# Forming the even heads of six groups like the odd ones in an attention kernel that shares its core with a Fourier layer

## The chip, the cores and the metric

One core of a Trainium2 chip runs the whole program. The metric is device time in microseconds (us), the median of several executions; a profile is one further execution, taken with the hardware profiler on. TensorE is written PE, VectorE DVE, ScalarE ACT, GpSimd POOL; SP is SyncE, which here does nothing but issue DMAs, in order.

## What is computed

Two independent layers, concatenated on the last axis. Part A is an attention with a compressive memory: 32 heads of width 18, four segments of 512 rows. Part B is a Fourier layer written as four dense products with DFT matrices.

```python
for s in range(N):                       # 4 segments of L = 512 rows
    logits = einsum("bhqd,bhkd->bhqk", qs, ks) * scale + mask     # causal
    p = softmax(logits)
    a_dot = einsum("bhqk,bhkd->bhqd", p, vs)
    a_mem = (phi(qs) @ M) / (phi(qs) @ z + 1e-6)
    outs.append(g * a_mem + (1 - g) * a_dot)
    M, z = M + phi(ks)^T @ vs, z + sum(phi(ks))
o = concat(outs) @ wo
a, b = x @ Re(Wd)^T, x @ Im(Wd)^T        # part B
y = Re(Ws) @ a - Im(Ws) @ b
```

## The kernel before, in words

All products keep nearly fp32 precision by splitting operands into a high and a low part. The program has three stages. In the first (about 0 to 240 us) the four segments are projected: q and k go to DRAM as three bf16 parts (`qd`, `kd`), v as `vd`, the memory's answer as `amd` (segments 1 to 3; `project_v` L309, `lookup` L390). In the second (about 240 to 930 us) two streams run side by side: `attention()` (L1138) and `dense()` (L668, the DFT products, matmuls at L583 and L628 to L633). In the third the output projection runs (`output_stage`, L868).

**Attention.** The 32 heads times 4 segments are 128 pieces, called heads here, numbered n, in 32 groups G of four (`G, h = divmod(n, 4)`); one group has one load of q and k stacks (`stack_load`), of values (`value_load`, L494) and of memory answers (`memory_load`, L1129). Scores of a head are four causal blocks of rows of 512, 384, 256 and 128 columns, 1280 in all. Heads come in pairs, an even one and an odd one, and the two are formed differently:

- An **even** head is formed *turned*. `s_fill` (L967) computes its scores in three parts (kinds 0: 512 columns; 1: 128 and 384; 2: 256) only so that DVE finds each row's maximum (`smallest`, L961, line L964). For the two even heads of a group POOL splits the maxima into three bf16 rows (`maxima`, L1005), PE turns them by an identity matmul (`maxima_transpose`, L1013, matmul L1015), ACT copies them (L1017), and two small DMAs put them as extra rows into the q stack. Then `t_fill` (L1021, matmuls L1032, L1035, L1040, L1041) computes the scores a second time, with keys on the partitions and the maximum already subtracted; ACT takes exp to fp16 (`hi`, L1044) and fp32 (`f`, L1045), POOL masks the diagonal blocks (`t_mask`, L1049), ACT copies the masked part to fp16 (`t_hi`, L1054), and DVE and POOL form the rest `lo` (`t_lo`, L1059). The result has the layout that the value product `pv` (L1061) needs.
- An **odd** head is formed *row by row*: `f_fill` (L973) computes the scores once and finds the maxima; `f_exp` (L980) adds a constant to the bias on ACT (L984) and takes exp with the row's bias (L987); `f_split_hi` (L989, L994) copies to fp16 on ACT; `f_split_lo` (L996, L998) forms the rest, 768 columns on POOL and 512 on DVE; `f_turn` (L1000, L1003) turns the 20 blocks of 128x128 with one DMA transpose issued by SP.

**Order.** Every engine runs its instructions in program order, and that order is written by hand. Iteration p of `attention()` has eight slots (L1153 to L1200, separated by `yield SLOTS[i]`; slot i below is the code ahead of the i-th yield, slot 0 the first). It handles the maxima of even head 2p, `t_fill` of even head 2(p-3), `f_fill` of odd head 2(p-2)+1, and `pv` of the heads of pair p-4. After every slot the main loop (L1209) takes as many pieces of the dense stream as keep the two streams at the same share of their planned totals; the plan's numbers (`SLOTS`) are fixed. `later(n, ...)` puts a DMA or a small step n slots on.

| slot | before: attention work in program order |
|---|---|
| 0 | `t_lo` part 0 of pair p-4; odd head: `f_exp` 2, `f_split_hi` |
| 1 | `s_fill` 0; `t_fill` 0 and 1 (and, every second iteration, the turned maxima in the columns that `t_fill` 1 leaves free); odd `f_split_lo` on POOL |
| 2 | `s_fill` 1; odd `f_split_lo` on DVE |
| 3 | `pv` of the even head; `s_fill` 2; `t_mask` |
| 4 | odd `f_fill` 1; `t_fill` 2; odd `f_fill` 0; `maxima` |
| 5 | odd `f_turn`; `stack_load`; copies in DRAM; `t_hi` |
| 6 | `pv` of the odd head; odd `f_fill` 2, `f_exp` 1; `t_lo` 1 and 2 |
| 7 | odd `f_exp` 0; `pv_out` |

**PSUM.** Score tiles use four banks in two pairs, `t` and `s`, each pair used in turn (`bank`, L564). `t_fill` 0, 1, 2 and the odd `f_fill` 0 take the `t` banks, `s_fill` 0, 1, 2 and the odd `f_fill` 1, 2 the `s` banks. A bank is free again when ACT has read it (for `s_fill`, DVE). The dense stream has three banks `d`; ACT copies finished ones out (L651, L634), and ACT and POOL also split each loaded DFT chunk (`c_cut`, L444: ACT L451, POOL L456).

Of the kernel before, what the change touches and what calls it, by code (L numbers as in the profile page):

```python
# [12 lines left out]
F32 = mybir.dt.float32  # L13
F32R = mybir.dt.float32r
F16 = mybir.dt.float16
# [20 lines left out]
COPIES = ((0, 3, 2, 0), (1, 3, 2, 2), (0, 5, 1, 0), (1, 5, 1, 1))  # L36
COPY_ROWS = 144


@with_exitstack  # L40
def infini_attention_and_fnet(ctx: ExitStack, tc: tile.TileContext, xT, wqk, w8, wv, wo, beta, xtT, cT, hT, out):
# [9 lines left out]
    kd = [dram.tile([D, 6, L], BF16, name=f"kd{s}") for s in range(NSEG)]  # L51
    vd = [dram.tile([P, 4, 8, 220], BF16, name=f"vd{s}") for s in range(NSEG)]
    amd = [dram.tile([4, P, D], F32, name=f"amd{s}") for s in range(NSEG)]
    yd = [dram.tile([P, D], F32, name=f"yd{t}") for t in range(NT)]
# [254 lines left out]
    def project_v(s, j, meanwhile):  # L309
# [26 lines left out]
        pool.tensor_tensor(vs[:, :, 0:18], r, vs[:, :, 36:54], OP.subtract)  # L336
        later(1, dma, vd[s][:, j], vs.rearrange("p (g h) c -> p g (h c)", g=8))

# [51 lines left out]
    def lookup(s, j):  # L390
# [26 lines left out]
        pool.tensor_tensor(am, nd[:, :, :DH], w.to_broadcast([P, H, DH]), OP.mult)  # L417
        later(1, dma, amd[s][j], am.rearrange("p h d -> p (h d)"))
        yield
# [73 lines left out]

    def value_load(G):  # L494
        if G < NG:
            s, g8 = divmod(G, 8)
            VS[G] = sa.tile([P, 4, 220], BF16, name="vst", bufs=2)
            dma(VS[G], vd[s][:, :, g8])

# [196 lines left out]
    def right_operands():  # L696
# [108 lines left out]
        for t, tag in ((1, "phi"), (9, "plo")):  # L805
            at(67, 4, o_load, t, lambda tag=tag: sa.tile([P, 5, P], F32, name="oraw", tag=tag, bufs=2))
        at(67, 4, lambda: list(left(0)))
# [165 lines left out]
    def f_fill(n, kind):  # L973
        o = scores(n, kind, "s" if kind else "t")
        if kind == 1:
            F_[n] = [sa.tile([P, 4], F32, name="nb", bufs=2), sa.tile([P, 1280], F32, name="pf", bufs=3), {}]
        smallest(o, kind, -SCALE, F_[n][0])
        F_[n][2][kind] = o
# [10 lines left out]
    def f_split_hi(n):  # L989
        f = F_[n][1]  # L990
        hl = sa.tile([P, 2, 1280], F16, name="hl", bufs=2)
        F_[n][2] = hl
        for a, b in ((512, 1280), (0, 512)):
            act.activation(hl[:, 0, a:b], f[:, a:b], AF.Copy)  # L994
# [5 lines left out]
    def f_turn(n):  # L1000
        hl = F_.pop(n)[2]
        PT[n] = sa.tile([P, 20, P], F16, name="ptt", bufs=2)
        nc.sync.dma_start_transpose(PT[n], hl.rearrange("p a c -> p (a c)"))  # L1003
# [17 lines left out]
    def t_fill(n, kind, maxima_of=None):  # L1021
        G, h = divmod(n, 4)
        q, k = qs_bufs[G % 4][:NPAIR + 3, h], ks_bufs[G % 4][:NPAIR + 3, h]
        if kind == 0:
            PT[n] = (sa.tile([P, 1280], F16, name="phi", bufs=2), sa.tile([P, 1280], F16, name="plo", bufs=2),
                     sa.tile([P, 1280], F32, name="pf", bufs=3))
        hi, lo, f = PT[n]
# [33 lines left out]
    def pv(n):  # L1061
# [4 lines left out]
        for i in range(4):  # L1066
            o = PV[n // 2][:, (h % 2 * 4 + i) * 55:(h % 2 * 4 + i + 1) * 55]
            for j in range(i + 1):
                if h % 2:
# [59 lines left out]
    def memory_load(G):  # L1129
        if 8 <= G < NG:  # L1130
            s, g8 = divmod(G, 8)
            dma(OG[G % 2], amd[s][:, :, 72 * g8:72 * g8 + 72].rearrange("q p c -> p q c"))

    F_LAG, T_LAG, V_LAG = 2, 3, 4
    NP = 2 * NG
    SLOTS = (1060.0, 890.0, 1060.0, 660.0, 890.0, 1060.0, 650.0, 1210.0)

    def attention():  # L1138
        for p in range(NP + V_LAG):
            def even(lag, fn, *a):  # L1140
                if 0 <= p - lag < NP:
                    fn(2 * (p - lag), *a)

            def odd(lag, fn, *a):
# [33 lines left out]
            odd(F_LAG, f_fill, 0)  # L1178
            if p % 2 and p < NP:
                maxima(p // 2)  # L1180
# [95 lines left out]
```

## Time and profile before

| | |
|---|---|
| median of 3 runs | 993.28 us (992.91 to 994.52) |
| the profiled execution's own time | 994.13 us |
| its span, first to last instruction | 992.4 us |
| granted TensorE clock | 0.999 |
| DMA moved | 209.97 MB, 212 GB/s |
| HBM read, written | 122.37 MB, 58.98 MB |

How to read it: the profile is of one execution on one core. "Busy" is the time in which an engine had an instruction in flight; matmuls overlap, so what one costs PE is seen from start to start and not from its duration. The 40 digits are tenths of busy time in equal slices of 24.8 us. "DMA share" is the mean time that the packets of the 16 DMA engines took, over the length of the stretch; it can go over 1, as packets overlap. A row of the timeline has start, length, engine, line, operation, output <- input, shapes, and in brackets the idle time before it with what ended that. A row of waits has the total, the number and the longest.

### The profile page before, as it was taken

The numbers are of one execution on the slowest core, as the hardware profiler recorded it, in microseconds if no ns is written. First come the engines' busy times: TensorE is split into PE (matmuls) and PEld (weight loads), VectorE is DVE, ScalarE is ACT, GpSimd is POOL, SyncE is SP. The second block draws the span as 40 slices with busy tenths as digits, with TensorE's granted clock in tenths as the row PEclk, the third lists the DMA queues.
The fourth block names the chain that finished last, engine by engine and source line by source line (L and its number), as shares of the span: only waits on it lengthen the run. The fifth ranks groups of instructions, "written<-read, shape, count | busy, mean of one in ns | idle before, by whom it ended". The sixth has DMA issues, their size and how long they took to land.

```text
span 992.4 us, 25495 instructions
## 1 busy us (share of the span) xinstructions
PE 980.9 (99%) x9246; PEld 918.3 (93%) x9246; DVE 786.4 (79%) x2115; ACT 714.7 (72%) x1687; POOL 675.2 (68%) x744
## 2 busy tenths in 40 slices
PE   9999999999999999999999999999999999999998
PEld 8988989898999999999999999999999999999998
DVE  6657668584678787887898878888888898989985
ACT  6757576563888777877878788886777778788442
POOL 2657576686676667676775777767676667887561
PEclk9999999999999999999999999999999999999999
DMA  7537556777578898899999998779999999988663
GB/s 241 191 117 244 194 170 241 238 243 214 146 179 206 224 239 227 203 226 241 223 253 242 235 211 191 187 196 218 247 231 219 224 241 252 249 200 180 168 199 112
DMA packets 304351, 209.97 MB, mean 212 GB/s; under 512 B 204992, under 2 KB 259136, under 8 KB 304192
## 3 DMA queue, kind: packets, MB, share of 16 engines
q1 hardware_dynamic: 304000, 208.20, 80.9%
q8 instruction: 72, 1.18, 0.5%
q14 instruction: 55, 0.45, 0.1%
q10 hardware_dynamic: 224, 0.14, 0.0%
HBM read 122.37 MB, written 58.98 MB: 183 GB/s over the span
## 4 chain that ended last, share of the span: by engine, by line
PE 84%; DVE 7%; ACT 4%; DMA 2%; issue 2%; POOL 1%; SPq 0%; POOLq 0%; DVEq 0%; ACTq 0%
PE d L583 38%; PE s L958 7%; PE v L84 4%; PE pv L1076 4%; PE qk L250 4%; PE d L628 3%; PE d L629 3%; PE d L630 3%; PE t L861 2%; PE pv L1077 2%; PE m L363 1%; PE d L861 1%; PE s L861 1%; PE t L1032 1%; PE qk L84 1%
## 5 line engine op out<-in xcount | busy, mean ns | idle before, releaser
L964 DVE CUSTOM_DVE_ANT_0 s<-s,causal 128x128 f32<-128x128 f32 (+3 forms) x512 | 248.4, 503 | 94.2 <-PE s L958 85.0
L456 POOL TENSOR_TENSOR clo<-craw,chi 128x512 fp32r<-128x512 f32 x158 | 218.2, 1381 | 91.1 <-ACT chi L451 60.8
L583 PE MATMUL d<-wide,chi 128*128 128x288 f32 x1408 | 261.9, 303 | 0.2 <-DVE y L653 0.2
L583 PEld LDWEIGHTS d<-wide,chi 128*128 128x128 f32 x1408 | 210.6, 188 | 2.7 <-issue 0.7
L583 PE MATMUL d<-wide,clo 128*128 128x288 f32 x704 | 173.4, 313 | 0.0
L998 POOL TENSOR_TENSOR hl<-pf,hl 128x768 f16<-128x768 f32 x64 | 114.0, 1782 | 67.4 <-ACT hl L994 55.6
L958 PE MATMUL s<-ks,qs 108*128 108x128 bf16 (+3 forms) x512 | 132.9, 303 | 1.7 <-DVE negm L964 1.2
L1044 ACT ACTIVATE phi<-t 128x384 f16<-128x384 f32 x128 | 61.8, 483 | 100.1 <-PE t L1041 100.1
L987 ACT ACTIVATE pf<-s,nb 128x128 f32<-128x128 f32 (+3 forms) x256 | 128.3, 527 | 6.2
L583 PE MATMUL d<-ab,chi 128*128 128x288 f32 x640 | 123.3, 302 | 0.0
L1059 DVE TENSOR_TENSOR plo<-pf,phi 128x384 f16<-128x384 f32 (+1 forms) x128 | 122.3, 955 | 0.0
L583 PEld LDWEIGHTS d<-wide,clo 128*128 128x128 f32 x704 | 117.8, 189 | 1.4
L1045 ACT ACTIVATE pf<-t 128x384 f32<-128x384 f32 (+1 forms) x192 | 99.6, 519 | 6.6 <-PE t L1032 6.3
L451 ACT ACTIVATE chi<-craw 128x512 fp32r<-128x512 f32 x160 | 100.1, 626 | 4.0 <-DMA craw<-xtT 2.4
L583 PEld LDWEIGHTS d<-ab,chi 128*128 128x128 f32 x640 | 97.8, 188 | 0.5
L994 ACT ACTIVATE hl<-pf 128x768 f16<-128x768 f32 (+1 forms) x128 | 87.4, 729 | 2.0
L583 PE MATMUL d<-ab,clo 128*128 128x288 f32 x320 | 83.0, 308 | 0.0
L628 PE MATMUL d<-wide,chi 128*128 128x288 f32 x256 | 81.4, 318 | 0.0
L630 PE MATMUL d<-wide,clo 128*128 128x288 f32 x256 | 75.6, 296 | 0.9 <-POOL clo L456 0.9
L629 PE MATMUL d<-wide,chi 128*128 128x288 f32 x256 | 75.6, 295 | 0.0
L1059 POOL TENSOR_TENSOR plo<-pf,phi 128x384 f16<-128x384 f32 x64 | 61.7, 963 | 12.0 <-ACT pf L1045 9.1
L998 DVE TENSOR_TENSOR hl<-pf,hl 128x512 f16<-128x512 f32 x64 | 69.2, 1081 | 0.0
(285 smaller groups left out, 2521.9 us busy)
## 6 DMA issues: line engine op xcount, KB each, us to landing
craw<-cT SPq DMA_DIRECT2D x128, 256.0 KB
ks<-kd SPq DMA_DIRECT2D x32, 432.0 KB
qs<-qd SPq DMA_DIRECT2D x32, 432.0 KB
craw<-xtT SPq DMA_DIRECT2D x32, 320.0 KB
vd<-vs SPq DMA_DIRECT2D x16, 440.0 KB
vst<-vd SPq DMA_DIRECT2D x32, 220.0 KB
qd<-p SPq DMA_DIRECT2D x16, 384.0 KB
kd<-p SPq DMA_DIRECT2D x16, 384.0 KB
```

The source lines that it names most:

```text
L451: act.activation(hi, raw[:, :4], AF.Copy)
L456: engine.tensor_tensor(lo, raw[:, :4], hi.bitcast(F32), OP.subtract)
L583: pe.matmul(o[h], a, b[:, h * 288:h * 288 + 288], start=start, stop=stop)
L628: pe.matmul(o, xh[:, k], wl[k][:, cs], start=k == 0, stop=False)
L629: pe.matmul(o, xh[:, k], wh[k][:, cs], start=False, stop=False)
L630: pe.matmul(o, xl[:, k], wh[k][:, cs], start=False, stop=False)
L958: pe.matmul(o[:, c:c + w], q[:, i * P:w], k[:, :w], start=True, stop=True)
L964: dve.tensor_tensor_reduce(o[:, c:c + w], o[:, c:c + w], CAUSAL[0][:, L - w:], scale=scale, scalar=-LOWEST, op0=OP.add, op1=OP.min, accum_ ...
L987: act.activation(f[:, FIRST_COL[i]:FIRST_COL[i] + w], o[:, c:c + w], AF.Exp, bias=nb[:, i:i + 1], scale=-1.0)
L998: engine.tensor_tensor(hl[:, 1, a:b], f[:, a:b], hl[:, 0, a:b], OP.subtract)
L1045: act.activation(f[:, r:r + w], o[:, :w], AF.Exp, bias=LIFT, scale=SCALE)
L1059: (pool if kind == 2 else dve).tensor_tensor(lo[:, a:b], f[:, a:b], hi[:, a:b], OP.subtract)
```

## The change

For the even heads of six of the 32 groups (G = 1, 3, 5, 7, 16, 18; twelve heads) the row-by-row way takes the place of the turned one. `s_fill`, `maxima`, `maxima_transpose`, `t_fill`, `t_mask`, `t_hi`, `t_lo` are not run for them; `f_fill`, `f_exp`, `f_split_hi`, `f_split_lo` and `f_turn` are, in iteration p = n/2 + 3, in the `t` banks alone. `pv` of such a head moves from slot 3 to slot 6. The following turned group's maxima, which stood beside `t_fill` 1 in slot 1, now stand beside the 256 columns of the new `f_fill` 2 in slot 4. The fp16 parts `phi` and `plo` become one tile, which also takes the DMA transpose of these heads. `vd` (segments 0 to 2) and `amd` (segments 1 and 2) are laid out so that a group's load is one contiguous piece per partition; the stores get eight pieces per partition instead of one.

```diff
+ROWWISE_GROUPS = (1, 3, 5, 7, 16, 18)
...
-    vd = [dram.tile([P, 4, 8, 220], BF16, name=f"vd{s}") for s in range(NSEG)]
-    amd = [dram.tile([4, P, D], F32, name=f"amd{s}") for s in range(NSEG)]
+    vd = [dram.tile([P, 8, 4, 220] if s < 3 else [P, 4, 8, 220], BF16, name=f"vd{s}") for s in range(NSEG)]
+    amd = [dram.tile([P, 8, 4, 72] if s < 3 else [4, P, D], F32, name=f"amd{s}") for s in range(NSEG)]
...
     def f_fill(n, kind):
-        o = scores(n, kind, "s" if kind else "t")
-        if kind == 1:
+        o = scores(n, kind, "s" if kind and n % 2 else "t")
+        if n not in F_:
...
     def f_split_hi(n):
         f = F_[n][1]
-        hl = sa.tile([P, 2, 1280], F16, name="hl", bufs=2)
+        hl = (sa.tile([P, 2, 1280], F16, name="hl", bufs=2) if n % 2
+              else sa.tile([P, 2, 1280], F16, name="hle", tag="pf", bufs=3))
...
-        PT[n] = sa.tile([P, 20, P], F16, name="ptt", bufs=2)
+        PT[n] = sa.tile([P, 20, P], F16, name="ptt", tag="ptt" if n % 2 else "phl", bufs=2)
...
-            even(T_LAG + 1, t_lo, 0)
+            turned(T_LAG + 1, t_lo, 0)
             odd(F_LAG + 1, f_exp, 2)
             odd(F_LAG + 1, f_split_hi)
             yield SLOTS[0]
-            G = p // 2 - 1 if p % 2 == 0 and 0 < p <= NP else None
-            even(0, s_fill, 0)
-            even(T_LAG, t_fill, 0)
-            even(T_LAG, t_fill, 1, G)
+            rowwise(T_LAG + 1, f_turn)
+            rowwise(T_LAG, f_fill, 0)
+            rowwise(T_LAG, f_fill, 1)
+            G = p // 2 - 1 if p % 2 == 0 and 0 < p <= NP and p // 2 - 1 not in ROWWISE_GROUPS else None
+            turned(0, s_fill, 0)
+            turned(T_LAG, t_fill, 0)
+            turned(T_LAG, t_fill, 1, G)
...
             odd(F_LAG + 1, f_split_lo, pool, 512, 1280)
             yield SLOTS[1]
-            even(0, s_fill, 1)
+            turned(0, s_fill, 1)
             odd(F_LAG + 1, f_split_lo, dve, 0, 512)
+            rowwise(T_LAG, f_exp, 0)
             yield SLOTS[2]
-            even(V_LAG, pv)
-            even(0, s_fill, 2)
-            even(T_LAG, t_mask)
+            turned(V_LAG, pv)
+            turned(0, s_fill, 2)
+            turned(T_LAG, t_mask)
+            rowwise(T_LAG, f_exp, 1)
             yield SLOTS[3]
             odd(F_LAG, f_fill, 1)
-            even(T_LAG, t_fill, 2)
+            turned(T_LAG, t_fill, 2)
+            rowwise(T_LAG, f_fill, 2)
+            if G is not None and 2 * (p - T_LAG) in ROWWISE:
+                maxima_transpose(G, F_[2 * (p - T_LAG)][2][2])
             odd(F_LAG, f_fill, 0)
-            if p % 2 and p < NP:
+            if p % 2 and p < NP and p // 2 not in ROWWISE_GROUPS:
                 maxima(p // 2)
             yield SLOTS[4]
...
-            even(T_LAG, t_hi)
+            turned(T_LAG, t_hi)
+            rowwise(T_LAG, f_exp, 2)
+            rowwise(T_LAG, f_split_hi)
             yield SLOTS[5]
+            rowwise(V_LAG, pv)
             odd(V_LAG, pv)
             odd(F_LAG, f_fill, 2)
+            rowwise(T_LAG, f_split_lo, pool, 512, 1280)
+            rowwise(T_LAG, f_split_lo, dve, 0, 512)
             odd(F_LAG, f_exp, 1)
-            even(T_LAG, t_lo, 1)
-            even(T_LAG, t_lo, 2)
+            turned(T_LAG, t_lo, 1)
+            turned(T_LAG, t_lo, 2)
             yield SLOTS[6]
```

`turned(...)` calls its function for even heads outside the six groups, `rowwise(...)` for those inside; `SLOTS` is unchanged.

More of the change, by code (lines that the diff above doesn't have):

```diff
@@ L336, in project_v @@
         pool.tensor_tensor(vs[:, :, 0:18], r, vs[:, :, 36:54], OP.subtract)
-        later(1, dma, vd[s][:, j], vs.rearrange("p (g h) c -> p g (h c)", g=8))
+        later(1, dma, vd[s][:, :, j] if s < 3 else vd[s][:, j], vs.rearrange("p (g h) c -> p g (h c)", g=8))
     started = set()
@@ L417, in lookup @@
         pool.tensor_tensor(am, nd[:, :, :DH], w.to_broadcast([P, H, DH]), OP.mult)
-        later(1, dma, amd[s][j], am.rearrange("p h d -> p (h d)"))
+        if s < 3:
+            later(1, dma, amd[s][:, :, j], am.rearrange("p (g h) d -> p g (h d)", g=8))
+        else:
+            later(1, dma, amd[s][j], am.rearrange("p h d -> p (h d)"))
         yield
@@ L497, in value_load @@
             VS[G] = sa.tile([P, 4, 220], BF16, name="vst", bufs=2)
-            dma(VS[G], vd[s][:, :, g8])
+            dma(VS[G], vd[s][:, g8] if s < 3 else vd[s][:, :, g8])
     for s in range(NSEG):
@@ L804, in right_operands, with second @@
                 "p a x -> p (a x)")[:, :5 * P].rearrange("p (k x) -> p k x", k=5))
-        for t, tag in ((1, "phi"), (9, "plo")):
-            at(67, 4, o_load, t, lambda tag=tag: sa.tile([P, 5, P], F32, name="oraw", tag=tag, bufs=2))
+        both = []
+        def second():
+            both.append(sa.tile([P, 2, 5, P], F32, name="oraw", tag="phl", bufs=2))
+            for i in range(2):
+                o_load(1 + 8 * i, lambda: both[0][:, i])
+        at(67, 4, second)
         at(67, 4, lambda: list(left(0)))
@@ L1024, in t_fill @@
         if kind == 0:
-            PT[n] = (sa.tile([P, 1280], F16, name="phi", bufs=2), sa.tile([P, 1280], F16, name="plo", bufs=2),
-                     sa.tile([P, 1280], F32, name="pf", bufs=3))
+            t = sa.tile([P, 2, 1280], F16, name="phl", bufs=2)
+            PT[n] = t[:, 0], t[:, 1], sa.tile([P, 1280], F32, name="pf", bufs=3)
         hi, lo, f = PT[n]
@@ L1068, in pv @@
             for j in range(i + 1):
-                if h % 2:
+                if h % 2 or n in ROWWISE:
                     b = FIRST_COL[i] // P + j
@@ L1131, in memory_load @@
             s, g8 = divmod(G, 8)
-            dma(OG[G % 2], amd[s][:, :, 72 * g8:72 * g8 + 72].rearrange("q p c -> p q c"))
+            dma(OG[G % 2], amd[s][:, g8] if s < 3 else amd[s][:, :, 72 * g8:72 * g8 + 72].rearrange("q p c -> p q c"))
     F_LAG, T_LAG, V_LAG = 2, 3, 4
     NP = 2 * NG
+    ROWWISE = {4 * G + h for G in ROWWISE_GROUPS for h in (0, 2)}
     SLOTS = (1060.0, 890.0, 1060.0, 660.0, 890.0, 1060.0, 650.0, 1210.0)
@@ L1142, in even, with turned, rowwise @@
                     fn(2 * (p - lag), *a)
+            def turned(lag, fn, *a):
+                if 2 * (p - lag) not in ROWWISE:
+                    even(lag, fn, *a)
+            def rowwise(lag, fn, *a):
+                if 2 * (p - lag) in ROWWISE:
+                    even(lag, fn, *a)
             def odd(lag, fn, *a):
```

## The prediction

> **What bounds the kernel now.** First the page's DMA digits for the whole span, then a table of stretches: PE is the bound, and in the stage where the change sits it has no idle time at all.
>
> ```profile
> DMA  7537556777578898899999998779999999988663
> ```
>
> ```profile
> 265.00:440.00 175.00, 175.00 (x1904) 164.97 (x1903) 137.32 (x413) 139.16 (x333) 122.91 (x136) 1.00 0.86 217
> 440.00:600.00 160.00, 159.95 (x1723) 150.36 (x1721) 138.83 (x401) 130.32 (x312) 114.00 (x127) 1.00 1.00 232
> 600.00:670.00 70.00, 70.00 (x735) 66.39 (x734) 56.93 (x174) 57.07 (x143) 51.05 (x59) 1.00 0.79 191
> ```
>
> The columns are PE, PE's weight loads, DVE, ACT and POOL in us (with counts), clock, DMA share, GB/s. Between 265 and 670 us, where groups 0 to 20 are formed, PE is busy 404.95 of 405 us. So time falls only by what PE no longer does, and every new wait of PE is paid in full. ACT (80 to 82%), DVE (78 to 87%) and the DMA (0.79 to 1.00) have some slack, and the waits of the same stretch say where ACT's is:
>
> ```profile
> ACT phi L1044 <- PE t L1041: 51.9, 35, 2.5
> ```
>
> An iteration takes about 10 us, so 405 us hold some forty. ACT's spare time is one gap per iteration (35 times, 1.5 us each), always ahead of `t_fill` 2 in slot 4. ACT waits there for PE: ACT is ahead of PE, by that much.
>
> **PE: what goes.** Timeline of iteration 10, PE:
>
> ```profile
> 331.20 0.39 PE L1032 MATMUL t<-qs,ks 111*128 111x128 bf16 x4
> 331.43 0.33 PE L1035 MATMUL t<-qs,ks 111*128 111x384 bf16 x1
> 331.59 0.22 PE L1015 MATMUL t<-ident,mb 128*128 128x128 bf16 x1
> 331.62 0.51 PE L583 MATMUL d<-wide,clo 128*128 128x288 f32 x2
> ...
> 333.81 0.20 PE L1076 MATMUL pv<-vst,phi 128*128 128x55 bf16 x1
> ...
> 334.33 0.27 PE L958 MATMUL s<-ks,qs 108*128 108x256 bf16 x1
> ...
> 335.20 0.22 PE L1040 MATMUL t<-qs,ks 111*128 111x128 bf16 x1
> 335.26 0.27 PE L1041 MATMUL t<-qs,ks 111*128 111x256 bf16 x1
> 335.37 0.38 PE L958 MATMUL s<-ks,qs 108*128 108x512 bf16 x1
> ```
>
> From start to start: `t_fill` 0 takes 0.23, `t_fill` 1 0.16, `t_fill` 2 0.06 + 0.11: 0.56 us for a head's 1280 columns. A changed head computes its scores once instead of twice: `f_fill` stands where `t_fill` stood, and `s_fill`, the same 1280 columns, goes. Twelve heads free 12 x 0.56 = 6.7 us; six turned maxima (L1015, 0.03 each) another 0.2. Some insertions into the dense stream vanish altogether (slots 2 and 3); no row prices that, I bound it by 0 and 1 us and take 0.1. **PE is freed of 7.0 us** (6.7 to 7.9).
>
> **ACT: what comes, and where.** The odd head in the same timeline runs just the code that the changed even heads get:
>
> ```profile
> 335.57 0.49 ACT L1044 ACTIVATE phi<-t 128x384 f16<-128x384 f32 x1 [1.41 <-PE t L1041]
> ...
> 336.91 0.62 ACT L451 ACTIVATE chi<-craw 128x512 fp32r<-128x512 f32 x1
> 337.43 0.19 ACT L984 ACTIVATE nb<-nb 128x2 f32<-128x2 f32 x1
> ...
> 338.38 0.20 ACT L984 ACTIVATE nb<-nb 128x1 f32<-128x1 f32 x1
> 338.62 0.69 ACT L987 ACTIVATE pf<-s,nb 128x512 f32<-128x512 f32 x1
> 339.34 0.20 ACT L984 ACTIVATE nb<-nb 128x1 f32<-128x1 f32 x1
> ...
> 340.08 1.37 ACT L994 ACTIVATE hl<-pf 128x768 f16<-128x768 f32 x2
> 341.36 0.62 ACT L451 ACTIVATE chi<-craw 128x512 fp32r<-128x512 f32 x1
> 341.88 0.58 ACT L1045 ACTIVATE pf<-t 128x512 f32<-128x512 f32 x1
> 342.35 0.48 ACT L1044 ACTIVATE phi<-t 128x384 f16<-128x384 f32 x1
> ```
>
> By starts: `f_exp` 1 takes 0.95, `f_exp` 0 0.83 (0.24, and 0.59 from 329.57 to 330.16 below), `f_exp` 2 0.74, `f_split_hi` 1.28, a DFT chunk's copy 0.52. A row-by-row head so costs ACT 3.8 us; a turned one costs 0.47 and twice some 0.37 in slot 1 (from 341.88) and 336.91 - 335.57 = 1.34 in slots 4 and 5, together 2.55. ACT gets 1.2 us more per changed head, against a gap of 1.5 us. In the mean this fits. But the gap lies ahead of slot 4, and the additions do not: `f_exp` 0 and 1 grow the work before it by 0.6 only, whereas `f_exp` 2 with `f_split_hi` (2.02 instead of 1.34) come behind it and ahead of the odd head's `f_exp` 1 and 0, which free PSUM banks. Nor can they start where `t_fill` 2's exps did. Those needed PE alone; `f_exp` 2 needs DVE's maximum, which in DVE's order stands behind the odd head's 128 and 384:
>
> ```profile
> 335.40 0.30 DVE L964 CUSTOM_DVE_ANT_0 s<-s,causal 128x128 f32<-128x128 f32 x1 [0.27 <-PE s L958]
> 335.79 0.57 DVE L964 CUSTOM_DVE_ANT_0 s<-s,causal 128x384 f32<-128x384 f32 x1
> 336.28 0.73 DVE L964 CUSTOM_DVE_ANT_0 s<-s,causal 128x512 f32<-128x512 f32 x1
> ...
> 338.81 0.43 DVE L964 CUSTOM_DVE_ANT_0 s<-s,causal 128x256 f32<-128x256 f32 x1 [1.39 <-PE s L958]
> ```
>
> The 256 columns would be reduced at 336.28 and ready at 336.71, not at 335.57: 1.14 us later. ACT then frees the odd `f_fill` 0's bank 1.14 + 0.68 = **1.8 us later**.
>
> *First wait: next iteration, slot 1.* Its second `t` fill needs exactly that bank. Its slack today is read twice: here `f_exp` 0 ends at 338.62 + 0.69 = 339.31 and the fill comes at 341.46; one iteration earlier 330.26 against 331.43.
>
> ```profile
> 329.57 0.69 ACT L987 ACTIVATE pf<-s,nb 128x512 f32<-128x512 f32 x1
> 330.16 0.19 ACT L984 ACTIVATE nb<-nb 128x1 f32<-128x1 f32 x1
> ...
> 341.46 0.33 PE L1035 MATMUL t<-qs,ks 111*128 111x384 bf16 x1
> ```
>
> Slack 2.15 and 1.17, against 1.8: a wait of 0 to 0.65. In the first iteration of each changed group (p = 2G + 3) the next group's turned head still has its `s_fill`, so DVE reduces twelve blocks, not eight. DVE's busy 137.32 of 175 us is 7.85 per 10; a head's reductions are, from the four rows above, 0.30 + 0.57 + 0.73 + 0.43 = 2.0: with the two `lo` parts about equal, DVE comes to 9.9 of 10 and runs up to 1 us late. Bounds 0 and 1.65; I take **0.7**, near the middle, as neither slack is rarer.
>
> *Second wait: that iteration's slot 4.* The odd `f_fill` 0 takes the bank of the changed head's `f_fill` 1. Once ACT is late, it has to do, after the odd `f_exp` 0: odd `f_exp` 2 and split (0.74 + 1.28), a chunk (0.52), `f_exp` 0 (0.83), `f_exp` 1 (0.95): 4.3 us. PE needs 335.37 - 331.43 = 3.94 for the same way today, and less after the change: `pv` of the even head, 0.52 (333.81 to 334.33), moves out of slot 3 behind slot 4, and for groups 1, 3, 5 and 16 the pair at slots 2 and 3 is itself a changed one without `s_fill` 1 and 2 (0.33). So 3.1 to 3.4: a wait of 1.2 or 0.9, none if ACT were on time and no chunk fell there. I take **1.1**. PE's faster way is what exposes ACT. In the iteration after it the moved `pv` gives ACT 0.5 us back, and the turned heads restore the gap: it ends there.
>
> Per group 1.8 us, six groups **10.8 us** (0 to 17).
>
> **DVE and POOL: what goes.** The masks, one `lo` part of 384 and the maxima leave POOL, 768 columns of `f_split_lo` come; DVE loses `t_lo` 0 and 1 for one 512 part:
>
> ```profile
> L998 POOL TENSOR_TENSOR hl<-pf,hl 128x768 f16<-128x768 f32 x64 | 114.0, 1782 | 67.4 <-ACT hl L994 55.6 <-PE t L1035 6.0 <-PE t L1015 2.7
> L1059 POOL TENSOR_TENSOR plo<-pf,phi 128x384 f16<-128x384 f32 x64 | 61.7, 963 | 12.0 <-ACT pf L1045 9.1 <-DMA y<-yd 2.5
> L998 DVE TENSOR_TENSOR hl<-pf,hl 128x512 f16<-128x512 f32 x64 | 69.2, 1081 | 0.0
> ```
>
> POOL gets 1.78 - 0.96 = 0.82 at most per head, less masks and maxima, on 122.91 busy of 175 us; PE meets both engines only through ACT. Zero.
>
> **DMA and SP.** One more transpose per changed head:
>
> ```profile
> L1003 SPq DMA_TRANSPOSE ptt<-hl x64: 3037/3745/6270, 258.7 to 918.4; - x64
> L498 SPq DMA_DIRECT2D vst<-vd x32: 595/611/1136, 227.7 to 901.6; - x32
> L94 SPq DMA_DIRECT2D vd<-vs x16: 319/320/407, 43.0 to 226.8; - x16
> ```
>
> Eight of the twelve fall between 265 and 440 us: 8 x 3.75 = 30 us on a share of 0.86 (24.5 us free) gives 1.03; four near 600 to 670 give 1.00. The stretch 440 to 600 ran at 1.00 with PE whole, so the bytes alone cost 0. The new layouts make 20 stores of the first stage shorter-pieced and 40 loads longer-pieced. A store holds SP 0.32, a load in short pieces 0.61; at twice that, 20 x 0.9 = 18 us of SP spread over 240 us in which the DMA is far from full (digits 3 to 7), so 0, with 2 us as the upper end; the loads' gain is hidden too.
>
> The new `f_turn` makes SP wait in slot 1 for `f_split_lo`; behind it in SP's order stand chunk loads, which run four chunks ahead, and the maxima's two DMAs. These start with a matmul that moves from 331.59 to about 335.4, and must land by the next `t_fill` 0, 0.22 ahead of 341.46: 5.8 us instead of 9.6 for ACT's copy, SP and the transfer. A held SP (3.75) still fits; 0, and 1 us per group as the upper end.
>
> **Sum.** 994.13 (its own time; span 992.4 and 1.7 around it) - 7.0 + 10.8 = 997.9. The median stands 0.85 below the profiled execution: **997.0**.
>
> **Rivals.** *The waits stay covered; faster.* If DVE is not late and chunks fall elsewhere, the slack of 2.15 covers the 1.8, and ACT enters slot 1 on time; of 10.8 us then 0 to 4 remain, and the time is 986 to 990.5. For it: 35 gaps of 1.5 us, and an addition of 1.2 per head. Against it: the gap is not where the addition is. It decides at a release 1.2 us later instead of 1.8.
>
> *SP becomes the bound; slower still.* Iteration 10's queue:
>
> ```profile
> 335.16 3.71 SPq L1003 DMA_TRANSPOSE ptt<-hl  x1
> ...
> 341.56 0.37 SPq L441 DMA_DIRECT2D craw<-cT  x1
> ...
> 345.11 3.10 SPq L1003 DMA_TRANSPOSE ptt<-hl  x1
> ```
>
> Six issues, the first and the last shown, stand one behind the other from 335.16 to 341.93, 6.8 of the 9.95 us to the next transpose. A second transpose makes that 10.5, more than the iteration. The even head's `f_turn` is issued in slot 1 and its `pv` stands in slot 6, some 6 us on; an issue that starts 2 us late and holds 3.75 makes PE wait 1 to 1.5 us for each changed head: 12 to 18 us more, some of it instead of ACT's waits: 1002 to 1010. The Trainium skill, Perfetto Trace Analysis, What "DMA-bound" means, counts an issuing engine whose track is solid with DMA slices as a bound of its own; at 68% of its time it is not that yet.
>
> *DVE stands behind POOL; slower still.* POOL's and DVE's parts of `f_split_lo` are issued together in slot 6. If DVE's 512 part cannot run beside POOL's 768, it ends up to 1.78 us late instead of in the row's mean of 1.08, next iteration's reductions start about 1 us later, and the first wait is 1.7 instead of 0.7: 6 us more, 1003 (1000 to 1005). Against it: the odd heads' two parts are issued within one slot of each other already, and 1.08 is their mean. The Trainium skill, SBUF — State Buffer, SBUF: two separate sides, has this as a rule: DVE with two SBUF inputs and a POOL instruction that reads SBUF exclude each other for the whole instruction.
>
> *Nothing measurable*: waits of 6 to 8 us, 991.3 to 995.3.
>
> **How the numbers follow.** Forecast (995.3 to 1001) 0.42, covered waits 0.34, SP 0.08, DVE behind POOL 0.05, evened out 0.11. A measurement of this kernel tells 0.2%, 2 us, from no change: faster 0.34, same 0.11, slower 0.55. The range: 987 leaves out a twelfth of all at the bottom (the covered case with no wait left), 1004 most of SP's and a third of DVE's; the forecast's own is 995.3 to 1001.
>
> **What would show it.** Right: PE waits at the second `f_fill` of the changed groups' second iteration and at the odd `f_fill` 0 in slot 4, released by ACT, 1 to 3 us per group, none in other iterations; the gap ahead of L1044 gone there. PE loses 12 x 7 = 84 matmuls at L1032 to L1041 and six at L1015. Wrong: PE busy whole from 265 to 670 us and the span 7 us shorter; or waits at `pv` L1076 behind the transposes (then SP); or a stall in the first stage (then the layouts).

## The result, and the profile after

The changed kernel takes **1034.8 us** (median of 4 runs, 1029.89 to 1038.45) against 993.1 us before (992.68 to 994.52): ratio 1.0414, 95% interval 1.0369 to 1.0459. It is slower, by far more than the forecast of 997.0, and above the forecast's range of 987 to 1004.

The profiled execution took 1035.5 us, its span is 1033.7: 41.3 more than before. First the page: busy time of the engines, PE's 40 digits, its granted clock, the DMA, and the chain that ended last.

```profile
PE 987.4 (96%) x9156; PEld 922.4 (89%) x9156; DVE 785.2 (76%) x2103; ACT 726.6 (70%) x1717; POOL 664.8 (64%) x708
...
PE   9989999999989797979999999989999999999998
...
PEclk9989999999999999999999999989999999999999
DMA  7647758767789989899999999969999999988653
...
PE d L587 29%; PE s L968 5%; DMA ptt<-hle 4%; PE qk L251 4%; PE pv L1087 4%; PE qk L85 3%; PE v L85 3%; PE d L634 3%; PE d L632 2%; PE d L633 2%; PE t L871 2%; DVE s L974 2%; PE pv L1088 2%; PE d L871 1%; PE s L871 1%
```

PE's digits, which were nines, now hold three 7s in slices 13 to 17 (counted from 0, so between about 336 and 465 us). PEclk shows an 8 only in slices 2 and 26, where PE's digit is an 8 as well; in a slice of 25.8 us a shorter loss of clock doesn't show. PE has 90 matmuls fewer, as foreseen (84 and 6), yet is busy 987.4 us instead of 980.9. A new entry stands in the chain: `DMA ptt<-hle`, the even heads' transposes, with 4%. The stretches that the prediction read (busy time of each engine, clock, DMA share, GB/s; the third one ends later because the groups do):

```profile
265.00:440.00 175.00, 157.48 (x1599) 147.27 (x1598) 122.30 (x366) 130.01 (x313) 104.06 (x99) 0.97 0.93 214
440.00:600.00 160.00, 153.89 (x1674) 144.49 (x1673) 128.92 (x376) 125.80 (x297) 107.37 (x117) 0.99 1.02 230
600.00:680.00 80.00, 77.62 (x802) 73.93 (x799) 64.68 (x194) 66.05 (x171) 55.33 (x61) 1.00 0.96 213
```

PE, which had no idle time here, is idle for 17.5, 6.1 and 2.4 us. The other engines are busy less in these windows because less gets done in them (1599 matmuls instead of 1904 in the first); over the whole span ACT is busy 11.9 us longer than before (726.6 against 714.7), POOL 10.4 less, DVE about as long. What PE waited for in the whole span (us in total, times, longest):

```profile
PE pv L1087 <- DMA ptt<-hle: 14.3, 6, 4.0
PE s L1026 <- DVE nb L974: 12.2, 6, 3.2
PE qk L251 <- DVE xt L120: 3.3, 1, 3.3
PE s L968 <- ACT pf L997: 3.2, 7, 0.8
PE s L968 <- DVE negm L974: 2.3, 5, 0.8
```

L1087 is `pv`, L1026 the turned maxima's matmul, L251 the first stage's projection, L968 the score matmul; of the last row 1.2 us were there before. **The balance:** idle time grew from 11.5 (992.4 - 980.9) to 46.3 us, by 34.8, and the first four rows make 33.0 of it. Busy time grew by 6.5 although 7.0 were freed, so 13.5 came to it. These 13.5 us are matmuls at half clock. The granted clock says so without the balance: at 0.986 over 1033.7 us, 14.5 us are lost; before, at 0.999 over 992.4 us, it was 1.0. Short stretches behind the waits show where:

```profile
67.00:73.00 6.00, 6.00 (x18) 4.84 (x18) 2.30 (x6) 3.54 (x10) 4.23 (x12) 0.50 0.63 157
298.47:301.88 3.41, 1.46 (x13) 1.19 (x12) 2.65 (x10) 2.15 (x8) 1.35 (x2) 1.00 0.93 226
301.88:305.29 3.41, 3.41 (x17) 3.41 (x16) 0.62 (x4) 3.25 (x9) 2.24 (x2) 0.50 0.22 70
```

PEclk is 0.50 in the first and the third row, and 1.00 a few us on; in the second row PE waits. There are six such stretches. Before the change this occurred only at the very end.

**The maxima's wait.** PE and DVE around the first of them:

```profile
298.46 0.50 PE L968 MATMUL s<-ks,qs 108*128 108x128 bf16 x3
300.92 0.22 PE L1026 MATMUL s<-ident,mb 128*128 128x128 bf16 x1 [1.95 <-DVE nb L974]
```

```profile
299.48 0.29 DVE L974 CUSTOM_DVE_ANT_0 s<-s,causal 128x128 f32<-128x128 f32 x1
...
299.86 0.57 DVE L974 CUSTOM_DVE_ANT_0 s<-s,causal 128x384 f32<-128x384 f32 x1
...
300.34 0.47 DVE L974 CUSTOM_DVE_ANT_0 s<-s,causal 128x256 f32<-128x256 f32 x1
300.72 0.14 DVE L974 DVE_READ_ACCUMULATOR2_ANT nb<- 128x1 f32 x1
```

PE fills three score blocks from 298.46 on; its next instruction in order is the maxima's matmul into the free columns of the 256-column tile. DVE reduces that tile in place, as the third block in its order (128, 384, 256), and the matmul starts at 300.92, after the maximum is read at 300.72 + 0.14. The columns differ, but the tile is one, and `f_fill` 2 with its reduction is written ahead of `maxima_transpose`. PE meets DVE here, six times, for 1.4 to 3.2 us.

**The transposes' wait.** SP's queue and PE one iteration later:

```profile
303.71 3.98 SPq L1014 DMA_TRANSPOSE ptt<-hl  x1
...
311.16 4.08 SPq L1014 DMA_TRANSPOSE ptt<-hle  x1
```

```profile
314.45 0.68 PE L587 MATMUL d<-ab,chi 128*128 128x288 f32 x4
317.00 0.20 PE L1087 MATMUL pv<-vst,ptt 128*128 128x55 bf16 x1 [1.86 <-DMA ptt<-hle]
```

The even head's transpose (311.16) stands behind the odd one and four other issues and holds SP to 315.24; `pv`, which PE could have started 1.86 us sooner, starts at 317.00. Rows of the tile `ptt` and of `vd` (count; duration in ns: least, median, most):

```profile
L1014 SPq DMA_TRANSPOSE ptt<-hl x64: 3012/3808/6871, 264.0 to 959.9; - x64
L1014 SPq DMA_TRANSPOSE ptt<-hle x12: 3648/4639/6032, 293.6 to 697.6; - x12
```

```profile
L95 SPq DMA_DIRECT2D vd<-vs x16: 319/514/1162, 42.2 to 233.4; - x16
```

A transpose of an even head holds SP for 4.6 us (median), not the 3.75 that I took; a `vd` store in shorter pieces 0.51 instead of 0.32.

**Where ACT waits** between 265 and 670 us:

```profile
ACT phl L1055 <- PE t L1052: 28.2, 20, 2.5
ACT nb L994 <- DVE nb L974: 23.7, 10, 4.4
```

The gap ahead of `t_fill` 2 fell from 51.9 us in 35 to 28.2 in 20; each is still 1.4 us long, but the changed heads have no `t_fill` 2. ACT now waits for DVE's maxima as well, the forecast's mechanism. But it reaches PE only through the fourth row above, 3.2 us. Three of its seven waits stand at the forecast's first place, the second fill of slot 1 (294.53, 342.79 and 390.98, for 0.61, 0.31 and 0.32 us); none stands at the second, the odd `f_fill` 0 of the same iteration, which comes right behind the maxima's matmul.

### The profile page after: what moved, and what is told of

Read it like the earlier page. It is cut to its first block, busy times and chain, and to the rows that moved or that the text cites. A ratio compares the mean times of both kernels' runs of the same rounds, so it can differ in the third digit from the quotient of the medians.

```text
span 1033.7 us, 25339 instructions
## 1 busy us (share of the span) xinstructions
PE 987.4 (96%) x9156; PEld 922.4 (89%) x9156; DVE 785.2 (76%) x2103; ACT 726.6 (70%) x1717; POOL 664.8 (64%) x708
## 4 chain that ended last, share of the span: by engine, by line
PE 68%; DVE 10%; DMA 9%; ACT 5%; issue 4%; POOL 2%; SPq 1%; POOLq 0%; DVEq 0%; ACTq 0%
PE d L587 29%; PE s L968 5%; DMA ptt<-hle 4%; PE qk L251 4%; PE pv L1087 4%; PE qk L85 3%; PE v L85 3%; PE d L634 3%; PE d L632 2%; PE d L633 2%; PE t L871 2%; DVE s L974 2%; PE pv L1088 2%; PE d L871 1%; PE s L871 1%
## 5 line engine op out<-in xcount | busy, mean ns | idle before, releaser
L587 PEld LDWEIGHTS d<-wide,chi 128*128 128x128 f32 x1408 | 214.3, 191 | 3.9 <-DVE y L657 0.9
L997 ACT ACTIVATE pf<-s,nb 128x128 f32<-128x128 f32 (+3 forms) x304 | 152.4, 527 | 8.2
L968 PE MATMUL s<-ks,qs 108*128 108x128 bf16 (+3 forms) x512 | 128.6, 303 | 6.0 <-ACT pf L997 3.2
L1055 ACT ACTIVATE phl<-t 128x384 f16<-128x384 f32 x104 | 50.4, 484 | 77.0 <-PE t L1052 77.0
L1070 DVE TENSOR_TENSOR phl<-pf,phl 128x384 f16<-128x384 f32 x104 | 100.4, 965 | 0.0
L1056 ACT ACTIVATE pf<-t 128x512 f32<-128x512 f32 x156 | 81.3, 521 | 10.1 <-PE t L1043 8.9
L1009 DVE TENSOR_TENSOR hl<-pf,hl 128x512 f16<-128x512 f32 x64 | 73.2, 1143 | 6.1 <-ACT hl L1005 6.1
L968 PEld LDWEIGHTS <-qs 108*128 108x128 bf16 x512 | 39.5, 98 | 31.2 <-issue 16.8
```

The costliest lines, as they stand in the source:

```text
L587: pe.matmul(o[h], a, b[:, h * 288:h * 288 + 288], start=start, stop=stop)
L968: pe.matmul(o[:, c:c + w], q[:, i * P:w], k[:, :w], start=True, stop=True)
L997: act.activation(f[:, FIRST_COL[i]:FIRST_COL[i] + w], o[:, c:c + w], AF.Exp, bias=nb[:, i:i + 1], scale=-1.0)
L1009: engine.tensor_tensor(hl[:, 1, a:b], f[:, a:b], hl[:, 0, a:b], OP.subtract)
L1070: (pool if kind == 2 else dve).tensor_tensor(lo[:, a:b], f[:, a:b], hi[:, a:b], OP.subtract)
```

## The experiments

Line numbers are those of each kernel. Ratios are to runs of the kernel before on the same chip, whose medians lay between 993.1 and 994.5 us; differences between two experiments are those of their medians. Waits are those of one profiled execution each.

**The layouts alone**, put into the kernel before:

```diff
-        later(1, dma, vd[s][:, j], vs.rearrange("p (g h) c -> p g (h c)", g=8))
+        later(1, dma, vd[s][:, :, j] if s < 3 else vd[s][:, j], vs.rearrange("p (g h) c -> p g (h c)", g=8))
```

(and `amd`, with the loads to match)

> The kernel before with the new layouts of vd and amd alone; no head is formed otherwise. Theory A (the first stage pays for the stores in eight short pieces per partition: an input load stands behind them, PE waits 3.3 us for the split input and then runs 6.8 us at half clock): the dense stream starts 4 to 7 us later, 997 to 1000 us, nothing more in the attention stage. Theory B (the layouts are free and the 6.6 us of the first stage have another cause): 992 to 994 us.

996.48 us (10 runs), ratio 1.0021 (1.0011 to 1.0030). The layouts alone cost 2 us. Its profile shows no stall of the first stage, but it is of the fastest of the ten executions (993.3), so where the 2 us arise isn't seen.

**The change with the old layouts**, the same edit taken back:

> The changed kernel with the old layouts of vd and amd. Theory A: the first stage is as before (dense stream starts at 219 us), 4 to 7 us less than the changed kernel, 1027 to 1031 us. Theory C (the long pieces of the loads are what keeps the DMA from being overrun in the attention stage): the waits of pv for the transposes grow and eat the 5 us, 1033 to 1045 us.

1028.47 us, 1.0349 (1.0332 to 1.0366): some 6 us below the full change. That is the size of the stall at L251 (3.3) with its half clock (6 us and more, half of it lost), but it isn't shown to be it: of the four profiles with the new layouts, two have the stall (the changed kernel, and 2.3 us in the run with the earlier transpose below) and two don't, and the profile here, without it, is of the slowest of five executions (1036.07). `pv` waits 15.9 us in it, the maxima's matmul 12.2, as in the changed kernel. The layouts aren't the main cause.

**The maxima ahead of the reduction** (the rest as changed):

```diff
-    def f_fill(n, kind):
+    def f_fill(n, kind, maxima_of=None):
         o = scores(n, kind, "s" if kind and n % 2 else "t")
+        if maxima_of is not None:
+            maxima_transpose(maxima_of, o)
...
-            rowwise(T_LAG, f_fill, 2)
-            if G is not None and 2 * (p - T_LAG) in ROWWISE:
-                maxima_transpose(G, F_[2 * (p - T_LAG)][2][2])
+            rowwise(T_LAG, f_fill, 2, G)
```

> The changed kernel, with the turned maxima put into the bank ahead of DVE's reduction of the 256 columns instead of behind it. Theory A (the maxima's matmul waits 1.4 to 3.2 us for DVE, six times, 12.2 us; SP then stands with the maxima's DMAs and issues the transposes late): these waits go, the waits of pv shrink too, 1012 to 1023 us. Theory D (as predicted: ACT frees the odd heads' banks late; the wait for DVE only shows first): PE then waits for ACT at the odd fills in the same places, 1027 to 1036 us.

1021.17 us, 1.0276 (1.0261 to 1.0291). The waits:

```profile
PE pv L1089 <- DMA ptt<-hle: 16.7, 7, 4.2
PE s L968 <- ACT pf L999: 6.4, 11, 1.4
```

The maxima's 12.2 us are gone, the time falls by 13.6. (This profile has no stall at L251 either, though the layouts are the new ones, so a part of the 13.6 may be that.) ACT's wait doubles to 6.4 us, for now the forecast's second place shows, the odd `f_fill` 0 of slot 4, directly behind the maxima's matmul: 0.23 to 1.42 us in five of the six groups, the longest here:

```profile
624.54 0.38 PE L968 MATMUL s<-ks,qs 108*128 108x512 bf16 x1 [1.42 <-ACT pf L999]
```

In the changed kernel PE's wait for the maxima stands right ahead of it, and no wait shows there.

**The even transpose earlier**, in slot 7 of the head's own iteration, ahead of the next one's issues:

```diff
-            rowwise(T_LAG + 1, f_turn)
             rowwise(T_LAG, f_fill, 0)
...
             yield SLOTS[6]
+            rowwise(T_LAG, f_turn)
```

> The changed kernel, with the even heads' DMA transpose issued in slot 7 of their own iteration instead of slot 1 of the next, two slots earlier in SP's order. Theory A (the transposes are late because SP issues them late, behind seven other issues): the waits of pv, 14.3 us in six, go or fall under 4 us, and with them half of the times at half clock, 1013 to 1023 us. Theory E (the DMA engines are full, so the transposes land late wherever they stand): pv waits as before, 1030 to 1038 us.

1023.21 us, 1.0298 (1.0283 to 1.0313):

```profile
PE s L1026 <- DVE nb L974: 12.2, 6, 3.3
PE pv L1087 <- DMA ptt<-hle: 6.5, 5, 2.4
```

The wait at `pv` falls from 14.3 to 6.5 us, the time by 11.6.

**All three together:**

> The changed kernel with three things put right at once: old layouts, the turned maxima ahead of DVE's reduction, the even heads' transposes issued two slots earlier. Theory A (waits for the maxima 12.2, for late transposes 14.3, the layouts about 5, and the half clock that follows the longer waits, explain the loss): what is left are the waits for ACT (6 us in the run with the maxima put right) and a few us at pv against 7 us freed; 992 to 1001 us. Theory F (the twelve heads bring PE waits however they are ordered, because SP or ACT has no room): 1008 us or more.

1015.53 us, 1.0220 (1.0202 to 1.0237). Singly the three were worth 6, 13.6 and 11.6 us, together only 19.3:

```profile
PE pv L1086 <- DMA ptt<-hle: 13.3, 7, 3.9
PE s L965 <- ACT pf L996: 6.4, 11, 1.4
```

The wait at `pv` is back at 13.3. SP around the changed groups 1 and 3:

```profile
313.77 7.91 SPq L1013 DMA_TRANSPOSE ptt<-hl  x1
321.74 0.59 SPq L499 DMA_DIRECT2D vst<-vd  x1
...
325.68 3.82 SPq L1013 DMA_TRANSPOSE ptt<-hl  x1
...
345.76 3.75 SPq L1013 DMA_TRANSPOSE ptt<-hle  x1
```

From 313.77 to the end of the last row each issue begins within 0.2 us of the end of the one before; one transpose holds SP for 7.9 us. An order by hand can move a transpose, but PE without the other waits needs it sooner, and SP has no free place for it in these rows. The Trainium skill, Perfetto Trace Analysis, What "DMA-bound" means, counts such a solid track of the issuing engine as a bound of its own; this trace agrees. My theory that the three repairs restore the gain fell here.

**`f_fill` 2 ahead of the odd `f_fill` 1**, so that DVE reduces the 256 columns earlier (on top of all three):

```diff
+            rowwise(T_LAG, f_fill, 2, G)
             odd(F_LAG, f_fill, 1)
             turned(T_LAG, t_fill, 2)
-            rowwise(T_LAG, f_fill, 2, G)
```

> As the run with three things put right, and the even head's 256-column scores issued ahead of the odd head's 128 and 384 in slot 4, so that DVE reduces them 0.9 us earlier and ACT can start the exps and the split that stand ahead of the odd head's exps. Theory H (the waits of PE for ACT come from that order, as the prediction's first wait had it): they fall by about half, 2 to 4 us less than without it. Theory I (ACT is simply out of time in these iterations): no change beyond 1 us.

1015.77 us, 1.0221. ACT's wait goes from 6.4 to 5.3 us, `pv`'s from 13.3 to 14.6: no change.

**PE waits of known length in the kernel before**, to price one. A matmul whose output isn't used reads a tile that POOL has just set 4 to 32 times:

```diff
+            if p in HELD:
+                HOLD.append(sa.tile([P, P], BF16, name="hold", bufs=1))
+                for _ in range(HELD[p]):
+                    pool.memset(HOLD[-1], 0.0)
+                t_fill(2 * (p - T_LAG), 1, None, HOLD[-1])
```

> The kernel before, with PE made to wait at eleven places of the attention stage, each four iterations or more from the last, by an added matmul into the free columns of the turned fill that reads a tile which POOL first sets 4 to 32 times; no result changes. It measures what a wait of PE costs. Theory A (after a long enough gap the clock is granted by half for 3.4 us, so a wait of 2 us or more costs itself and 1.7 us, a wait under 1.5 us only itself): the time grows by the sum of the waits and 1.7 us for each half-clock stretch in the profile, and short waits show none. Theory G (the half-clock stretches of the changed kernel come from its different mix of work and not from gaps): no half-clock stretch here, and the time grows by the waits alone.

1046.13 us, 1.0537 (1.0513 to 1.0561). Nine waits came about, 35.3 us in all; the two shortest, and the clock behind them:

```profile
PE t L1039 <- POOL hold L1174: 35.3, 9, 6.7
```

```profile
484.65 0.23 PE L1039 MATMUL t<-ident,hold 128*128 128x128 bf16 x1 [1.43 <-POOL hold L1174]
```

```profile
568.66 0.23 PE L1039 MATMUL t<-ident,hold 128*128 128x128 bf16 x1 [2.25 <-POOL hold L1174]
```

```profile
478.00:487.00 9.00, 7.57 (x76) 6.95 (x76) 6.11 (x22) 7.16 (x17) 7.44 (x14) 1.00 1.11 230
```

```profile
569.50:572.50 3.00, 3.00 (x22) 2.70 (x22) 1.66 (x5) 0.81 (x2) 2.83 (x3) 0.50 0.44 169
573.00:574.00 1.00, 1.00 (x11) 0.89 (x9) 0.49 (x2) 0.00 (x0) 0.19 (x1) 1.00 0.41 80
```

Behind 1.43 us the clock stays at 1.00; behind 2.25 us it is 0.50 for some 3 us. The span grew by 49.0 (1041.4 against 992.4) for 35.3 of waits: in the mean of these nine, of 1.4 to 6.7 us, a wait of PE costs about 1.4 times itself.

**The transposes alone.** The kernel before, all heads formed as before; the odd heads' transposes of the six groups are issued a second time, into the same tile, in slot 1 of the next iteration, where the change puts the even ones:

```diff
+    def turn_again(n):
+        nc.sync.dma_start_transpose(PT[n], LAST.pop(n).rearrange("p a c -> p (a c)"))
...
+            if 2 * (p - V_LAG) in AGAIN:
+                odd(V_LAG, turn_again)
```

> The kernel before, all heads formed as before; only the DMA transpose of the odd heads of the six groups is issued a second time, into the same tile, in slot 1 of the next iteration: the place of the changed even heads' transpose, with the same deadline (pv in slot 6). ACT, DVE, POOL and PE have their old work, so this is the added transposes alone. Theory A (SP cannot issue a second transpose per iteration in time): PE waits at pv for the transposes 9 to 16 us in all, with some half-clock stretches, 1004 to 1016 us. Theory J (the transposes are late because the row-by-row heads finish late on ACT, DVE and POOL): pv waits under 3 us, 993 to 998 us.

1020.74 us, 1.0283 (1.0256 to 1.0310): **27 us for twelve transposes**, with PE, ACT, DVE and POOL doing what they did before.

```profile
PE pv L1081 <- DMA ptt<-hl: 20.9, 9, 4.1
```

**The same twelve without a deadline**, in slot 7, into the tile that `pv` of slot 6 is done with:

```diff
-        nc.sync.dma_start_transpose(PT[n], LAST.pop(n).rearrange("p a c -> p (a c)"))
+        nc.sync.dma_start_transpose(DONE[n], LAST[n + 2].rearrange("p a c -> p (a c)"))
```

> The kernel before, with the same twelve further transposes as in the run with repeated ones, but without a deadline: in slot 7 of an iteration the odd head that was just turned in slot 5 is turned once more, into the joint tile that pv of slot 6 has finished with, which nobody reads again. Nothing is left out; the extra result is not used. PE computes what it does in the kernel before. Theory L (the deadline): the transposes cost because pv in slot 6 stands behind each of them; without that deadline PE waits 0 to 3 us behind the transposes and the time is 993 to 998. Theory M (the load): twelve more transposes fill SP's queue so far that the ordinary transposes and chunk loads behind them are late too; PE waits over 6 us behind the DMA, some at half clock, and the time is 1003 or more. Between 998 and 1003: both, with the waits at pv in the trace as the part of the load.

1012.59 us, 1.0191 (1.0168 to 1.0214). `pv` hardly waits; something else does:

```profile
PE t L1037 <- DMA qs<-mt: 10.6, 5, 2.9
PE pv L1081 <- DMA ptt<-hl: 3.0, 3, 1.6
```

```profile
356.23 6.16 SPq L1003 DMA_TRANSPOSE ptt<-hl  x1
...
363.58 1.61 SPq L94 DMA_DIRECT2D qs<-mt  x2
```

```profile
365.92 0.61 PE L1037 MATMUL t<-qs,ks 111*128 111x128 bf16 x4 [2.89 <-DMA qs<-mt]
```

The turned maxima's two DMAs (363.58) stand behind a further transpose, and `t_fill` 0 comes 2.89 us late. So up to 18 of the 27 us stay when `pv` doesn't stand behind the further transposes: whatever is due next in the queue is late. (The further transposes also made SP itself wait for their tile, 6.6 us over six; that part belongs to this experiment only, so 18 is an upper end.)

**24 DRAM copies issued by POOL instead of SP** (on top of all three; the same bytes):

```diff
-                    later(2, copy_parts, 2, 8 + p // 2)
+                    later(2, copy_parts, 2, 8 + p // 2, pool.dma_start)
...
-                later(2, copy_parts, 3, (p - 4) // 2)
+                later(2, copy_parts, 3, (p - 4) // 2, pool.dma_start)
```

> As the run with three things put right, with the copies in DRAM of the attention stage (24 of 0.5 to 0.6 us on SP, one per iteration at most, none due soon) issued by POOL instead of SP. Theory A (SP's queue is the bound in the changed iterations): each changed iteration before iteration 36 gets 0.6 us of SP back, the pv waits of groups 3 to 7 fall by 2 to 5 us, 1009 to 1013 us, if POOL's own work is not held up. Theory C (the DMA engines' load is the bound): the copies load them as before, 1013 to 1017 us.

1011.6 us, 1.0183 (1.0168 to 1.0198), 3.9 less than with SP; `pv` waits 9.4 instead of 13.3. SP's queue is part of the limit; the rest may be the DMA engines, whose share is 0.9 to 1.0 here. These two weren't separated further.

**Twelve heads spread**, one in each of groups 1 to 8 and 16 to 19 (old layouts, early transposes, maxima turned as in the kernel before):

```diff
-    ROWWISE = {4 * G + h for G in ROWWISE_GROUPS for h in (0, 2)}
+    ROWWISE = {4 * G for G in (1, 2, 3, 4, 5, 6, 7, 8, 16, 17, 18, 19)}
```

> Twelve changed heads again, as many as in the changed kernel, but one in each of twelve groups (1 to 8 and 16 to 19). The same heads are freed of their second scores, the same number of transposes is added, and a second transpose comes in every second iteration instead of two in a row. Theory A (SP over two iterations: 14.1 us of issues and one more transpose of 3.75 us fit 20 us): pv waits of 0 to 3 us, ACT 2 to 4, 6.7 us freed: 988 to 995 us. Theory C (twelve more transposes cost what they cost, by the DMA engines' load): 1005 to 1016 us as without the spreading.

1021.38 us, 1.0273 (1.0257 to 1.0288); `pv` waits 13.4 us. Spreading doesn't help, though the expectation's count of SP, 14.1 + 3.75 us of issues in two iterations of 20, had room. That count took the added transpose at 3.75 us; here the twelve hold SP for 4.8 us in the median and up to 7.3. So a count with the old lengths doesn't explain the lateness, and what makes the transposes longer no run shows.

**Six heads**, one per group, and then **five**, without group 7 and with the copies on POOL:

```diff
+    ROWWISE = {4 * G for G in (1, 3, 5, 7, 16, 18)}
```

> As the run with three things put right, but only the first even head of each of the six groups is formed row by row, so that no two iterations in a row bring a second transpose; the maxima of every group are then turned as before. Theory A (SP's queue is the bound: an iteration with two transposes asks more than 10 us of it, and the second in a row finds it behind): the waits of pv for the transposes go to under 1 us in all, the waits for ACT to 1 to 2 us, six heads free 3.4 us: 990 to 994 us. Theory B (a changed head's transpose is late by itself, because five slots are too short for it): about half of the 13 us of pv waits stays, 997 to 1003 us.

> A version meant to be the best of these: one changed head in each of groups 1, 3, 5, 16 and 18 (without group 7, where the run with six single heads had its only wait for a transpose), old layouts, maxima and transposes put right, copies in DRAM issued by POOL. 2.8 us freed; the waits for ACT of the six-head run (about 3 us with the one at a dense bank) stay. Theory A (SP's lateness is gone, ACT's waits cancel what is freed): 992 to 995.5 us, no difference to the kernel before that counts. Theory K (a half-clock stretch or a wait turns up elsewhere): over 996 us.

998.34 us, 1.0042 (1.0030 to 1.0055), and 998.14 us, 1.0037 (1.0023 to 1.0051). With six heads `pv` waits once:

```profile
PE pv L1086 <- DMA ptt<-hle: 2.5, 1, 2.5
```

Half the heads free 3.4 us (6 x 0.56), but PE is idle 4.9 us longer than before (16.4 against 11.5) and its busy time falls by only 0.7. With five heads `pv` waits three times, 5.0 us in all, in a profile of the slowest of seven executions. No version here beats the kernel before.

## Why the prediction was wrong, point by point

- **Matmuls that go: right.** 90 fewer; 7.0 us fits the balance of busy time, with the half clock as the other term (13.5 us by the balance, 13.5 by the granted clock).
- **ACT's two waits, 10.8 us, the term of the forecast: mis-sized.** DVE's order and its late maximum are as drawn (299.48 to 300.86), and ACT waits for it, but PE lost 3.2 us by it, and 6.4 where the maxima's wait was taken away. The two places were the right ones: 0.31 to 0.61 us at the first, in three groups, for a forecast of 0.7 in six, and 0.23 to 1.42 at the second, in five, for a forecast of 1.1.
- **"So the bytes alone cost 0", and SP's queue as a rival with 0.08: the step that failed most.** The 8 x 3.75 us against 24.5 free was a sum over 175 us; it hid that the transposes come two to an iteration, with a due time each. The rival had the mechanism, its place and even its price (12 to 18 us at `pv`; 14.3 measured). The price fits partly by luck: it had 1 to 1.5 us for each of twelve heads, whereas six made PE wait, up to 4.0 us, and the time that it gave, 1002 to 1010, was too low, as the maxima and the half clock were missing from it too. Still, it should have been the forecast: its own row had SP at 6.8 + 3.75 = 10.5 us of a 9.95 us iteration, and what I set against it, a stretch at a DMA share of 1.00 with PE whole, says nothing of due times. The repeated transposes show 27 us for this alone, and up to 18 where `pv` doesn't stand behind them.
- **The maxima's move, "0, and 1 us per group as the upper end": failed.** I followed the two DMAs behind the matmul and not what stands ahead of it. 12.2 us of waits; the time fell by 13.6 us when the matmul was put ahead of the reduction.
- **The layouts, "0, with 2 us as the upper end": near for them alone** (2 us), but some 6 in the changed kernel, where the profile has a stall of 3.3 us at L251; that the stall is the 6 us stays open.
- **A wait priced at its length: failed.** Every term of the sum took a wait at itself. 13.5 us of the 41.3 are half clock behind waits.
- **DVE behind POOL: small.** DVE's 512 part of an even head takes 1.27 us in the mean (1.08 for an odd one before); no wait of PE in the table goes back to one of these. But in five of the six places where the maxima's matmul waited, DVE came to its reductions from an *odd* head's 512 part of 1.40 to 1.73 us (1.73 at 344.76, where POOL's 768 part of that head was still running for 1.2 us). Over the mean of 1.08 before this is 2.3 us of the 12.2 at most.

Terms by the trace, which add up to the change of the span: 14.3 (transposes) + 12.2 (maxima) + 3.3 (layouts) + 3.2 (ACT) + 1.8 (other idle time) + 13.5 (half clock) - 7.0 = 41.3.

## What to carry to other kernels

Count a full queue per iteration and by due time, not by its share over a stage: where one queue's issues add up to more than the iteration, something in it is late, and moving one issue makes another late. Take the lengths that the issues have once the new ones stand among them (4.8 us for a transpose here), not those of the kernel before (3.75). When an instruction is moved, look at what was last written to its tile, by whom, even in other columns. On an engine without idle time price a wait at more than its length.

## What the runs showed of the hardware

PE's clock halves behind some gaps and not behind others, and the length of the gap alone doesn't decide it. Behind 1.95 us (300.92 above) it was 0.50 for 3.41 us. Behind 2.38 us (635.02 to 637.40, changed kernel) and behind 3.13 us (306.75 to 309.88, the run with the maxima ahead) it stayed at 1.00:

```profile
632.98:636.39 3.41, 2.04 (x16) 1.73 (x15) 3.34 (x12) 3.29 (x10) 2.74 (x3) 1.00 1.08 109
636.39:639.80 3.41, 2.40 (x18) 2.37 (x18) 2.54 (x9) 1.45 (x6) 0.90 (x3) 1.00 0.85 194
```

```profile
309.88 0.20 PE L1089 MATMUL pv<-vst,ptt 128*128 128x55 bf16 x1 [3.13 <-DMA ptt<-hle]
```

```profile
304.77:308.18 3.41, 1.97 (x15) 1.74 (x14) 1.18 (x4) 3.35 (x10) 2.75 (x4) 1.00 1.00 199
308.18:311.60 3.42, 1.72 (x46) 1.73 (x47) 0.38 (x3) 0.47 (x1) 1.26 (x1) 1.00 0.99 221
```

The shorter slow stretches of the changed kernel begin at 301.88, 363.32, 411.11 and 458.90. These lie 61.44, 47.79 and 47.79 us apart, 18, 14 and 14 times 3.413, and each of them lasts 3.41 us. So the clock seems to be set on a raster of pieces of 3.41 us, and the windows above are cut along it. The 1.95 us fall into one piece of the raster (298.47 to 301.88, PE busy for 1.46 us of it), and the next piece is slow; a boundary splits the 2.38 us into 1.37 and 1.01 and the 3.13 us into 1.44 and 1.69, and no piece is slow. What counts by these traces is PE's idle time within one piece: 1.85 us were enough (the run with copies on POOL, 384.17 to 386.02), 1.69 weren't, and in between both occur. This was read from the traces afterwards; no run was made to test it. The Trainium skill, TensorE: Matmul & The Clock Gate, Part 1, lets the clock fall after an idle window of about 3.4 us, the windows running free. The length of the slow stretches and the raster agree; a window idle from end to end wasn't needed here, 1.85 us of one were enough.

A transpose of 128 x 2560 fp16 values holds SP between 3.0 and 7.9 us. The added ones hold it longer than the 3.75 of the kernel before: 4.6 us in the median in the changed kernel, 4.8 when the twelve are spread. What stretches a single one, the runs don't show.
